# Linear attention and a token-mixing MLP: third products moved, flips and output products on the whole TensorE array, stores held back

## The chip, the cores and the metric

The kernel runs on one core of one Trainium2 chip. A time is the device time of one execution in microseconds; a kernel's time is the median over its runs. A profile is one execution of the program recorded by the hardware profiler. In the profile PE is TensorE's matmul, PEld its weight load, DVE VectorE, ACT ScalarE, POOL GpSimd and SP SyncE, which here only issues DMAs.

## The reference

Two layers follow each other. The first is a causal linear attention with a decay per head, over 4 batches, 8 heads, 768 positions and 64 channels, in blocks of 64:

```
intra = (q k^T * lam^(i-j) for i >= j) v
inter = (q * lam^(i+1)) kv_state
out   = intra + inter
kv_state = lam^64 * kv_state + (k * lam^(63-j))^T v
```

The second takes the result as x [4, 768, 512] (the heads side by side) and mixes tokens:

```
wq = x w_q ; wk = x w_k                      # [4, 768, 64]
mixed = (wq wk^T / 8) x                      # over the 768 positions
out = relu(mixed) w_out                      # [4, 768, 512], float32
```

All inputs and the output are float32.

## The kernel before

The work is tiled into 16 **pairs** n = 0 to 15: batch b = n // 4 and two heads (kk = n % 4). The kernel works in chunks of 128 positions, six to a pair, with both heads packed on TensorE: head 0 on one half of the array's rows or columns, head 1 on the other. The decay is split into a factor on q and a factor on v, so that a mask of zeros and ones is all that is left of it between a query and a key. One iteration of the loop `for n in range(N)` (line 515) does, for pair n:

- `scores(n)` (L275): k^T q for each chunk, four PSUM tiles `sc`; two row halves of the array (the profile writes 64*128).
- `masks(n, a)` (L295): DVE multiplies two of these tiles by the mask, to `pr` in SBUF.
- `inter(n)` (L301): the product of the running state `gs` and the queries, into `oa` (quarters of the array, 64*64).
- `values(n)` (L318): v times `pr`, added into `oa` (two column halves, 128*64); ACT then copies `oa` to `xT`, x transposed.
- `states(n)` (L248): the running sums of k^T v of a pair (128*64), which DVE brings to SBUF as `gs`.
- `turn(n)` (L208): q and k of a coming pair are transposed on TensorE (128*64). DVE writes `qT`, ACT writes `kT`.
- `flip(n - 1)` (L344): `xT` of the pair before is transposed back, in 12 column halves, to `xp`; DVE (for batch 0 ACT) copies it to `xnat`.

When a batch is through, the token mixing of that batch is spread over the pairs of the next two: `mix_wk` (whole array, 128*128), `mix_wq` and `mix_py` (128*64), the third products `mix_pm` (four of them per batch, index dd), and six output products `mix_po` (index t, 128 positions each). A third product has two shapes: wide, two products on two row halves (64*128), or in quarters, four products on 64*64. Two PSUM tiles `pm` come out of it, and ACT applies the relu to both (`rmT`). An output product is eight matmuls in column halves; ACT copies its tile `po` to `osb`, and SP stores 256 KB.

Which of these stands where is written by hand: for each n the lists `rows` (third products ahead of the scores, wide), `quarters` (third products right behind `inter`), `one` (ahead of or behind the turning) and `two` (after `values` and `states`). `tc.manual_schedule()` keeps each engine's instructions in the order of the program. The order in an iteration is

```
before, n < 8:   rows | scores masks0 [wk] states masks1 flip | one turn | inter quarters | values [states] | two
before, n >= 8:  rows | scores masks0 [wk] masks1 | inter quarters | flip turn | one | values states | two
```

PSUM has six buffers that all tiles but `oa` share (`ps`, L51) and two for `oa` (`psx`). A tile that finds no free buffer waits for the evacuation of an earlier one. `osb` has four buffers (L50). Loads of q, k and v are POOL's (float32 in memory, bf16 in SBUF): iteration n issues those of pair n + 6 in the order q, k, scaling of v of pair n + 4 on POOL, v (L201). SP's queue holds, after the loads at the start, nothing but stores.

Of the kernel before, what the change touches and what calls it, by code (L numbers as in the profile page):

```python
# [27 lines left out]
def kernel(  # L28
# [18 lines left out]
    gsp = ctx.enter_context(tc.tile_pool(name="gsp", bufs=3))  # L47
    xtp = ctx.enter_context(tc.tile_pool(name="xtp", bufs=2))
    hyp = ctx.enter_context(tc.tile_pool(name="hyp", bufs=2))
    outp = ctx.enter_context(tc.tile_pool(name="outp", bufs=4))  # L50
    ps = ctx.enter_context(tc.tile_pool(name="ps", bufs=6, space=bass.MemoryType.PSUM))  # L51
    psx = ctx.enter_context(tc.tile_pool(name="psx", bufs=2, space=bass.MemoryType.PSUM))
    ctx.enter_context(tc.manual_schedule())
# [136 lines left out]
    def scale_v(n, eng):  # L190
        b, kk = pairs[n]
        vn = nat.tile([128, 2, NCH, D], BF16, tag="vn", name="vn")
        eng.tensor_tensor(  # L193
            out=vn,
            in0=staged.pop((n, "v")),
            in1=DvI[:, 2 * kk : 2 * kk + 2, :].unsqueeze(3).to_broadcast([128, 2, NCH, D]),
            op=ALU.mult,
        )
        L[n]["vn"] = vn
# [95 lines left out]
    def masks(n, a):  # L295
        for hl in range(2):
            t = prb.tile([128, 3, CH], BF16, tag="pr", name="pr")
            nc.vector.tensor_tensor(out=t, in0=L[n]["sc"][a, hl], in1=maskc, op=ALU.mult)  # L298
            L[n]["pr"][a, hl] = t
# [41 lines left out]
                nc.scalar.copy(out=to, in_=oa[a])  # L341
        del L[n]

    def flip(n):  # L344
        b, kk = pairs[n]
        xp = pst([128, NCH, CH], BF16, "xp")
        for t in range(NCH):
            for i in range(2):
                o = t * CH + i * 64
                nc.tensor.transpose(  # L350
                    xp[i * 64 : i * 64 + 64, t, :], xT[b][:, kk, o : o + 64], ident
                )
        to = xnat[b][:, :, kk * CH : (kk + 1) * CH]
        if b == 0 or n == N - 1:
            nc.scalar.copy(out=to, in_=xp)
        else:
            nc.vector.tensor_copy(out=to, in_=xp)
# [7 lines left out]
    def mix_wk(b, kts=range(NP)):  # L365
        if 0 in kts:
            M[b] = dict(wk=pst([128, NCH, DHY], F32, "wk"))
        wk = M[b]["wk"]
        for t in range(NCH):
            for kt in kts:  # L370
                nc.tensor.matmul(
                    wk[:, t, :],
                    xT[b][:, kt, t * CH : (t + 1) * CH],
                    wqk[:, 1, kt, :],
                    start=(kt == 0 and (t == 0 or len(kts) == NP)),
                    stop=(kt == NP - 1),
                    skip_group_check=True,
                )
        if NP - 1 in kts:
            wkn = hyp.tile([128, NCH, DHY], BF16, tag="wkn", name="wkn")  # L380
            nc.vector.tensor_copy(out=wkn, in_=wk)
            M[b]["wkn"] = wkn

    def mix_wq(b, kts=range(NP)):
        if 0 in kts:
            M[b]["wq"] = pst([128, HALF], F32, "wq")
        wq = M[b]["wq"]
        for kt in kts:
            for n in range(2):
                nc.tensor.matmul(  # L390
                    wq[n * 64 : n * 64 + 64, :],
                    wqk[:, 0, kt, :],
                    xT[b][:, kt, n * HALF : (n + 1) * HALF],
                    start=(kt == 0),
                    stop=(kt == NP - 1),
                    skip_group_check=True,
                )
        if NP - 1 in kts:
            wqT = hyp.tile([128, HALF], BF16, tag="wqT", name="wqT")
            nc.scalar.copy(  # L400
                out=wqT.rearrange("j (c p r) -> j c r p", c=3, r=2),
                in_=wq.rearrange("j (c r p) -> j c r p", c=3, r=2),
            )
            M[b]["wqT"] = wqT

    def mix_py(b, last=False):
        py = pst([128, 256], F32, "py")
        for t in range(NCH):
            for i in range(2):
                nc.tensor.matmul(  # L410
                    py[i * 64 : i * 64 + 64, :],
                    M[b]["wkn"][:, t, :],
                    xnat[b][:, t, i * 256 : i * 256 + 256],
                    start=(t == 0),
                    stop=(t == NCH - 1),
                    skip_group_check=True,
                )
        Y = hyp.tile([128, 2, 256], BF16, tag="Y", name="Y")
        nc.scalar.copy(out=Y[:, 0, :], in_=py)
        for i in range(2):  # L420
            o = slice(64 - i * 64, 128 - i * 64)
            if last:
                nc.vector.tensor_copy(out=Y[i * 64 : i * 64 + 64, 1, :], in_=py[o, :])
            else:
                nc.scalar.copy(out=Y[i * 64 : i * 64 + 64, 1, :], in_=py[o, :])
        M[b]["Y"] = Y
        M[b]["rmT"] = hyp.tile([128, 4, S], BF16, tag="rmT", name="rmT")

    def mix_pm(b, which, wide=True, engs=None):
# [20 lines left out]
        for i, ((dd, n), pm) in enumerate(zip(which, pms)):  # L450
# [10 lines left out]
            else:  # L461
                nc.scalar.activation(out=to, in_=pm, func=ACT.Relu, scale=1.0 / 8.0)  # L462

    def mix_po(b, t, last=False):
        cols = (256, 256) if last and t == NCH - 1 else (HD,)
        osb = outp.tile([128, HD], F32, tag="osb", name="osb")
        c = 0
        for w in cols:
            po = pst([128, w], F32, "po")
            for kt in range(4):  # L470
                for i in range(2):
                    o = t * CH + i * 64
                    nc.tensor.matmul(  # L473
                        po[i * 64 : i * 64 + 64, :],
                        M[b]["rmT"][:, kt, o : o + 64],
                        wo[:, kt, c : c + w],
                        start=(kt == 0),
                        stop=(kt == 3),
                        skip_group_check=True,
                    )  # L480
            if last and (c or (t % 2 and len(cols) == 1)):
                nc.vector.tensor_copy(out=osb[:, c : c + w], in_=po)  # L482
            else:
                nc.scalar.copy(out=osb[:, c : c + w], in_=po)  # L484
            (nc.scalar if len(cols) == 2 and c == 0 else nc.sync).dma_start(
                out=out[b, t * CH : (t + 1) * CH, c : c + w], in_=osb[:, c : c + w]
            )
            c += w


    warm(WARM2)
# [23 lines left out]
    for n in range(N):  # L515
        b, kk = pairs[n]
        if 8 <= n + 6 < N:
            load_more(n + 6)
        if n + 6 >= N and n + 4 < N:
            scale_v(n + 4, nc.gpsimd)  # L520
        if n == 1:
            load_wqk()
        if n == 3:
            nc.scalar.copy(out=wqk, in_=wqk_f)
        p = b - 1

        def po(b, *ts):
            return [lambda t=t: mix_po(b, t) for t in ts]

        rows, quarters, one, two = {
            4: ([], [], [lambda: mix_wq(0)], [lambda: mix_py(0)]),
            5: ([], [0, 1], [], []),
            6: ([2], [3], [], po(0, 0, 1)),
            7: ([], [], po(0, 2, 3), po(0, 4, 5)),
        }.get(n, ([], [], [], []))
        if b >= 2:
            rows, quarters, one, two = [
                ([], [], [lambda: mix_wq(p)], [lambda: mix_py(p)]),  # L540
                ([], [0], po(p - 1, 3) if b > 2 else [], po(p - 1, 4) if b > 2 else []),
                ([1], [2], po(p - 1, 5) if b > 2 else [], []),
                ([3], [], [], po(p, 0, 1, 2) if b < B - 1 else po(p, 0, 1)),
            ][kk]
        for dd in rows:
            mix_pm(p, dd)
        scores(n)
        masks(n, 0)
        if b >= 1 and kk == 0:
            mix_wk(p)  # L550
        if n < 8:

            states(n)
            masks(n, 1)
            if n >= 1:
                flip(n - 1)
            for f in one:
                f()
            turn(n + 1)
            if n == 0:  # L560
                scale_v(1, nc.vector)
                make_dq(2)
            if n == 1:
                make_dq(3)
        else:
            masks(n, 1)

        inter(n)
        for dd in quarters:
            mix_pm(p, dd, wide=False)  # L570
        if n >= 8:
            flip(n - 1)
            if 8 <= n <= 9:
                turn(n + 1)
            if n != 8 and n + 2 < N:
                turn(n + 2)
            for f in one:
                f()
        if n == N - 1:
            mix_wk(b, (0, 1, 2))  # L580
            mix_wq(b, (0, 1, 2))
        values(n)
        if n >= 7 and n + 1 < N:
            states(n + 1)
        for f in two:
            f()
    bl = B - 1
    mix_po(bl - 1, 2)
# [44 lines left out]
```

## Time and profile before

| what | value |
|---|---|
| median of 5 runs | 105.45 us (104.69 to 105.56) |
| profiled execution: own time, span | 105.45 us, 103.4 us |
| PE, PEld busy | 86.5 us, 60.3 us |
| DVE, ACT, POOL busy | 66.2 us, 63.8 us, 67.5 us |
| granted TensorE clock | 1.0 in all slices |
| scores(0) start, scores(8) start, last matmul starts | 9.1 us, 47.8 us, 99.5 us |

A busy PE means that some matmul was in flight, and a matmul on a half or a quarter of the array runs beside its partner. So what a block of matmuls costs TensorE is read from the start of its first matmul to the start of the next block. The timeline gives these starts; a bracket behind a line tells how long the engine stood before it and what ended that. Blocks are named by the tile that they write: `sc` scores, `oa` inter (64*64) and values (128*64), `xp` flip, `trq` and `trk` turning, `dps` states, `pm` third products, `po` output products.

### The profile page before, as it was taken

Reading aid. Unit: us, or ns where it says so; the run is one execution under the profiler, and the core shown is the slowest. Engines: PE = TensorE matmul, PEld = TensorE weight load, DVE = VectorE, ACT = ScalarE, POOL = GpSimd, SP = SyncE. Lnnn points to the kernel's source line nnn. Section 1 sums busy time; section 2 is a strip of 40 time slices with the busy share of each in tenths; the row PEclk is TensorE's granted clock in tenths of the full one; section 3 lists DMA queues with packets and bytes.
Section 4 is the critical chain, followed back from the end, with each engine's and each line's share of the span. In section 5 each row is a group of like instructions: output and inputs, shape, how many; then the busy total and the mean of one; then the engine's idle time right before and its main releaser. Section 6 shows DMA issues by size and latency. Waiting matters only on the chain. (4 is left out here: it accounts for less than half of the span.)

```text
span 103.4 us, 3945 instructions
## 1 busy us (share of the span) xinstructions
PE 86.5 (84%) x1714; PEld 60.3 (58%) x1714; DVE 66.2 (64%) x165; ACT 63.8 (62%) x126; POOL 67.5 (65%) x69
## 2 busy tenths in 40 slices
PE   4955887959886889999798698999899889999950
PEld 1324576746865565786675576768585565643530
DVE  3247998894847493864959399739857782264330
ACT  4283658946491869482397578653888824876430
POOL 5999999898999699999908999996041000000000
PEclk9999999999999999999999999999999999999999
DMA  0999999999999999999999999999903120733584
GB/s 23 267 173 156 163 171 159 175 166 163 195 176 164 164 153 163 124 245 263 199 218 218 158 164 137 136 157 288 153 10 142 67 101 0 270 139 133 220 312 148
DMA packets 67410, 17.15 MB, mean 166 GB/s; under 512 B 62914, under 2 KB 64450, under 8 KB 67394
## 3 DMA queue, kind: packets, MB, share of 16 engines
q0 software_dynamic: 60400, 9.57, 125.1%
q1 hardware_dynamic: 6850, 7.21, 21.4%
q8 instruction: 13, 0.21, 0.8%
q10 hardware_dynamic: 144, 0.13, 0.4%
q14 instruction: 3, 0.02, 0.1%
HBM read 20.19 MB, written 6.29 MB: 256 GB/s over the span
## 5 line engine op out<-in xcount | busy, mean ns | idle before, releaser
L298 DVE TENSOR_TENSOR pr<-sc,maskc 128x384 bf16<-128x384 f32 x64 | 32.0, 548 | 11.7 <-PE sc L285 11.7
L193 POOL TENSOR_TENSOR vn<-fv,DvI 128x768 bf16<-128x768 bf16 x14 | 20.9, 1494 | 9.2 <-DMA fv<-in_v_dram 8.4
L473 PE MATMUL po<-wo,rmT 128*64 128x512 bf16 (+1 forms) x200 | 23.0, 371 | 0.1
L242 ACT COPY kT<-trk 128x768 bf16<-128x768 bf16 x16 | 12.8, 799 | 13.8 <-PE trk L238 13.5
L484 ACT COPY osb<-po 128x512 f32<-128x512 f32 (+1 forms) x22 | 12.6, 582 | 9.9 <-PE po L473 6.0
L79 POOL DMA_DIRECT2D fv<-in_v_dram x16 | 17.3, 1079 | 0.8 <-POOLq L617 0.8
L79 POOL DMA_DIRECT2D fk<-in_k_dram x15 | 15.6, 1037 | 0.0
L473 PEld LDWEIGHTS <-rmT 128*64 128x64 bf16 x200 | 10.8, 110 | 8.0 <-ACT rmT L462 0.7
L341 ACT CAST xT<-oa 128x384 bf16<-128x384 f32 x31 | 13.5, 495 | 2.5 <-PE oa L329 2.5
L462 ACT ACTIVATE rmT<-pm 128x384 bf16<-128x384 f32 x28 | 12.3, 507 | 1.5 <-PE pm L442 1.5
L285 PE MATMUL sc<-qT,kT 64*128 64x128 bf16 x192 | 9.8, 217 | 3.8 <-ACT rmT L462 1.0
L74 POOL DMA_DIRECT2D fq<-in_q_dram x15 | 12.6, 843 | 0.0
L285 PEld LDWEIGHTS <-kT 64*128 64x128 bf16 x192 | 6.6, 94 | 7.7 <-issue 4.6
L225 DVE TENSOR_TENSOR qT<-trq,dq 128x768 bf16<-128x768 bf16 x16 | 8.8, 548 | 1.7 <-PE trq L219 1.7
L238 PE MATMUL trk<-ident,fk 128*64 128x128 bf16 x180 | 7.8, 220 | 2.3 <-DMA fk<-in_k_dram 2.3
L350 PE MATMUL xp<-ident,xT 128*64 128x128 bf16 x192 | 8.4, 221 | 1.0 <-ACT osb L484 0.6
L329 PE MATMUL oa<-pr,vn 128*64 128x128 bf16 x192 | 8.7, 221 | 0.5 <-DVE pr L298 0.5
L219 PE MATMUL trq<-ident,fq 128*64 128x128 bf16 x192 | 8.5, 220 | 0.7 <-ACT fq L501 0.6
L329 PEld LDWEIGHTS <-vn 128*64 128x64 bf16 x192 | 6.7, 109 | 2.5 <-issue 1.3
L308 PE MATMUL oa<-qT,gs 64*64 64x128 bf16 x160 | 7.8, 222 | 0.2
L265 DVE COPY two<-dps 128x64 f32<-128x64 f32 x16 | 3.5, 221 | 6.6 <-PE dps L255 6.5
L350 PEld LDWEIGHTS <-xT 128*64 128x64 bf16 x192 | 6.3, 110 | 2.3 <-issue 1.7
(59 smaller groups left out, 113.2 us busy)
## 6 DMA issues: line engine op xcount, KB each, us to landing
out_dram<-osb SPq DMA_DIRECT2D x23, 256.0 KB, 2.1
fv<-in_v_dram POOLq DMA_DIRECT2D x16, 192.0 KB, 6.6
fq<-in_q_dram POOLq DMA_DIRECT2D x15, 192.0 KB, 7.1
fk<-in_k_dram POOLq DMA_DIRECT2D x15, 192.0 KB, 7.5
wo<-in_moe_w_out_dram POOLq DMA_DIRECT2D x1, 512.0 KB, 9.1
k<-in_k_dram SPq DMA_DIRECT2D x1, 384.0 KB, 3.7
q<-in_q_dram SPq DMA_DIRECT2D x1, 384.0 KB, 4.8
wqk_f<-in_moe_w_q_dram SPq DMA_DIRECT2D x1, 128.0 KB, 6.7
```

The costliest lines, as they stand in the source:

```text
L74: nc.gpsimd.dma_start(out=t, in_=q_rows(n))
L79: nc.gpsimd.dma_start(out=t, in_=kv_rows(n, dict(k=k, v=v)[nm]))
L193: eng.tensor_tensor(out=vn, in0=staged.pop((n, "v")), in1=DvI[:, 2 * kk : 2 * kk + 2, :].unsqueeze(3).to_broadcast([128, 2, NCH, D]), op=A ...
L242: nc.scalar.copy(out=kT, in_=trk)
L285: nc.tensor.matmul(sc[a, hl][:, cc, :], kT[r, c * CH : (c + 1) * CH], qchunk(n, r, c), start=True, stop=True, skip_group_check=True,)
L298: nc.vector.tensor_tensor(out=t, in0=L[n]["sc"][a, hl], in1=maskc, op=ALU.mult)
L329: nc.tensor.matmul(oa[a][r, cc, :], vn[:, hl, c, :], pr[a, hl][:, cc, :], start=False, stop=(cc == 2), skip_group_check=True,)
L341: nc.scalar.copy(out=to, in_=oa[a])
L350: nc.tensor.transpose(xp[i * 64 : i * 64 + 64, t, :], xT[b][:, kk, o : o + 64], ident)
L462: nc.scalar.activation(out=to, in_=pm, func=ACT.Relu, scale=1.0 / 8.0)
L473: nc.tensor.matmul(po[i * 64 : i * 64 + 64, :], M[b]["rmT"][:, kt, o : o + 64], wo[:, kt, c : c + w], start=(kt == 0), stop=(kt == 3), ski ...
L484: nc.scalar.copy(out=osb[:, c : c + w], in_=po)
```

## The change

Four things are changed.

- Third products: the list `rows` is gone. All stand behind `inter`, in quarters: dd 0 and 1 in the pair kk = 1, dd 2 and 3 in the pair kk = 2 (for batch 0 in pairs 5 and 6).
- Output products: a whole-array form, four matmuls of 128 output rows in place of eight on column halves, everywhere. In the loop they stand ahead of `inter` (list `whole`), and for batch 0 all in pairs 7 and 8 (before: 6 and 7).
- Flips: in the pairs from 8 on they stand right behind the scores, the masks and `mix_wk`, and `flip` makes six transposes on the whole array. The flips called in pairs 1 to 7 keep the column halves (`halves=True`). `flip(N - 1)` at the end is whole too.
- Stores: `mix_po` notes its store in a list, and `store()` issues what is noted. For batch 0 nothing is issued at once. At n = 8 SP issues a small DMA that reads v of pair 14 from its staging tile, and so waits until that load has landed; the stores noted so far follow, and the other two of batch 0 go with the first one of batch 1. `osb` gets 14 buffers.

The order in an iteration becomes

```
after, n < 8:   scores masks0 [wk] whole states masks1 flip [wq] turn | inter quarters | values [states] | cols
after, n >= 8:  scores masks0 [wk] masks1 flip whole | inter quarters | turn [wq] | values states | cols
```

where `cols` holds `mix_py` alone.

```diff
-    outp = ctx.enter_context(tc.tile_pool(name="outp", bufs=4))
+    outp = ctx.enter_context(tc.tile_pool(name="outp", bufs=14))
...
-    def flip(n):
+    def flip(n, halves=False):
         b, kk = pairs[n]
         xp = pst([128, NCH, CH], BF16, "xp")
         for t in range(NCH):
-            for i in range(2):
-                o = t * CH + i * 64
-                nc.tensor.transpose(
-                    xp[i * 64 : i * 64 + 64, t, :], xT[b][:, kk, o : o + 64], ident
-                )
+            w = 64 if halves else CH
+            for i in range(0, CH, w):
+                o = t * CH + i
+                nc.tensor.transpose(xp[i : i + w, t, :], xT[b][:, kk, o : o + w], ident)
...
+    stores = []
+
+    def store():
+        while stores:
+            b, t, c, w, osb = stores.pop(0)
+            (nc.scalar if w < HD and c == 0 else nc.sync).dma_start(
+                out=out[b, t * CH : (t + 1) * CH, c : c + w], in_=osb[:, c : c + w]
+            )
+
     def mix_po(b, t, last=False):
...
             for kt in range(4):
-                for i in range(2):
-                    o = t * CH + i * 64
-                    nc.tensor.matmul(
-                        po[i * 64 : i * 64 + 64, :],
-                        M[b]["rmT"][:, kt, o : o + 64],
-                        wo[:, kt, c : c + w],
-                        start=(kt == 0),
-                        stop=(kt == 3),
-                        skip_group_check=True,
-                    )
+                nc.tensor.matmul(
+                    po,
+                    M[b]["rmT"][:, kt, t * CH : (t + 1) * CH],
+                    wo[:, kt, c : c + w],
+                    start=(kt == 0),
+                    stop=(kt == 3),
+                )
...
-            (nc.scalar if len(cols) == 2 and c == 0 else nc.sync).dma_start(
-                out=out[b, t * CH : (t + 1) * CH, c : c + w], in_=osb[:, c : c + w]
-            )
+            stores.append((b, t, c, w, osb))
             c += w
+        if b > 0:
+            store()
...
+        if n == 8:
+
+            late = consts.tile([1, D], BF16, name="late")
+            nc.sync.dma_start(out=late, in_=staged[n + 6, "v"][0:1, 0, 0, :])
+            store()
...
-        rows, quarters, one, two = {
-            4: ([], [], [lambda: mix_wq(0)], [lambda: mix_py(0)]),
-            5: ([], [0, 1], [], []),
-            6: ([2], [3], [], po(0, 0, 1)),
-            7: ([], [], po(0, 2, 3), po(0, 4, 5)),
-        }.get(n, ([], [], [], []))
-        if b >= 2:
-            rows, quarters, one, two = [
-                ([], [], [lambda: mix_wq(p)], [lambda: mix_py(p)]),
-                ([], [0], po(p - 1, 3) if b > 2 else [], po(p - 1, 4) if b > 2 else []),
-                ([1], [2], po(p - 1, 5) if b > 2 else [], []),
-                ([3], [], [], po(p, 0, 1, 2) if b < B - 1 else po(p, 0, 1)),
+        whole, quarters, cols = {
+            4: ([], [], [lambda: mix_py(0)]),
+            5: ([], [0, 1], []),
+            6: ([], [2, 3], []),
+            7: (po(0, 0, 1, 2, 3), [], []),
+            8: (po(0, 4, 5), [], [lambda: mix_py(p)]),
+        }.get(n, ([], [], []))
+        if n > 8:
+            whole, quarters, cols = [
+                ([], [], [lambda: mix_py(p)]),
+                (po(p - 1, 3) if b > 2 else [], [0, 1], []),
+                (po(p - 1, 4, 5) if b > 2 else [], [2, 3], []),
+                (po(p, 0, 1, 2) if b < B - 1 else po(p, 0, 1), [], []),
             ][kk]
-        for dd in rows:
-            mix_pm(p, dd)
         scores(n)
         masks(n, 0)
+
         if b >= 1 and kk == 0:
             mix_wk(p)
+        if n >= 8:
+            masks(n, 1)
+            flip(n - 1)
+        for f in whole:
+            f()
         if n < 8:
 
             states(n)
             masks(n, 1)
             if n >= 1:
-                flip(n - 1)
-            for f in one:
-                f()
+                flip(n - 1, halves=True)
+            if kk == 0 and b:
+                mix_wq(p)
             turn(n + 1)
...
-        else:
-            masks(n, 1)
 
         inter(n)
         for dd in quarters:
             mix_pm(p, dd, wide=False)
         if n >= 8:
-            flip(n - 1)
             if 8 <= n <= 9:
                 turn(n + 1)
             if n != 8 and n + 2 < N:
                 turn(n + 2)
-            for f in one:
-                f()
+            if kk == 0:
+                mix_wq(p)
...
         values(n)
         if n >= 7 and n + 1 < N:
             states(n + 1)
-        for f in two:
+        for f in cols:
             f()
```

## The prediction

> **What bounds the kernel now.** I read the page first, then the timeline of PE from 34 us on, then that of ACT, DVE and POOL beside each stall.
>
> ```profile
> PE 86.5 (84%) x1714; PEld 60.3 (58%) x1714; DVE 66.2 (64%) x165; ACT 63.8 (62%) x126; POOL 67.5 (65%) x69
> ...
> PE   4955887959886889999798698999899889999950
> ...
> DMA  0999999999999999999999999999903120733584
> ```
>
> No engine is full, PE is nearest, and the DMA engines are full for the first three quarters. So PE's order of work sets the time, with holes in it. An undisturbed stretch of PE's timeline gives the price of the blocks and of a change of array form:
>
> ```profile
> 68.47 0.51 PE L285 MATMUL sc<-qT,kT 64*128 64x128 bf16 x12
> 68.91 0.87 PE L371 MATMUL wk<-wqk,xT 128*128 128x64 bf16 x24
> 69.71 0.47 PE L308 MATMUL oa<-qT,gs 64*64 64x128 bf16 x10
> 70.11 0.53 PE L350 MATMUL xp<-ident,xT 128*64 128x128 bf16 x12
> 70.47 0.50 PE L219 MATMUL trq<-ident,fq 128*64 128x128 bf16 x12
> ```
>
> From start to start: scores 0.44, wk 0.80, inter 0.40, a flip 0.36. Within `sc` a pair of matmuls follows the last after 0.053, so six pairs are 0.32, and 0.12 is the change of form behind them. The 24 wk start 0.0295 apart, 0.71, which leaves 0.09; inter costs 0.30 where a 64*64 block follows (53.72 to 54.02) and 0.40 here. A change of form is 0.10.
>
> The holes, from pair 6 to 15:
>
> ```profile
> 50.13 0.53 PE L350 MATMUL xp<-ident,xT 128*64 128x128 bf16 x12 [0.62 <-ACT osb L484]
> ...
> 57.40 0.53 PE L238 MATMUL trk<-ident,fk 128*64 128x128 bf16 x12 [0.73 <-DMA fk<-in_k_dram]
> ...
> 59.57 0.34 PE L285 MATMUL sc<-qT,kT 64*128 64x128 bf16 x5 [0.29 <-DVE gs L267]
> ...
> 74.52 0.35 PE L442 MATMUL pm<-wqT,Y 64*64 64x384 bf16 x3 [0.32 <-ACT Y L425]
> ...
> 83.13 0.32 PE L285 MATMUL sc<-qT,kT 64*128 64x128 bf16 x5 [0.80 <-ACT rmT L462]
> ```
>
> Most are scores that stop halfway. Six PSUM buffers go round, the row-shaped third product ahead of the scores takes two, and the last scores need a buffer that ACT or DVE still empties.
>
> **The change part by part.** I add the starts of the blocks up pair by pair, before and after. The loop from the third product at 35.51 to the end of the output products of pair 15 (two of the three from 85.71, so 87.42) takes 51.9 us; 44.6 of it are blocks at their undisturbed price, 7.3 are waits.
>
> *Third products.* A row one costs 0.17 (62.36 to 62.53), one in quarters 0.16 (inter with it 79.30 to 79.86, 0.56, less 0.40). PE gains nothing by the shape. The scores behind rows took 0.98, 0.95, 0.95, 0.87 and 1.44 in pairs 6, 10, 11, 14, 15 against 0.44, and the flip of pair 6 waited 0.46 for `rmT`: 3.5 us of the 7.3 go. The third products of pairs 9 and 13 stand 0.6 and 0.7 waiting for `Y`; a flip (and in 13 an output product) now covers most of that. With the smaller holes of pairs 10 and 11 these are 1.7 us. With 0.7 and 1.4 further down that is the 7.3.
>
> What is late next: two third products in one pair take four buffers at once. In pairs 9 and 10 the second to fourth wait for masks, and `trk` for the evacuation of the flip. DVE does four masks in 1.95 us from 0.38 behind the scores, and `xnat` after them (53.66 to 56.07 behind scores at 53.28), so `trk` can't start before 2.8 us into the pair; by its blocks PE is there after 1.9 (0.44, flip 0.43, inter 0.40, 0.32, `trq` 0.33). That is 0.9 twice. In pair 13 the output product behind the flip takes the buffer that the copies to `Y` free, 1.3 us in (73.13 to 74.46) where PE is there after 0.9: 0.4, so 2.2 us. Pair 6 gets what pair 5 has now, 1.30 for inter and two third products (33.75 to 35.05) against 0.72, and DVE's chain of masks, states, masks, flip, `qT` behind it: 0.9.
>
> *Flips and output products.* The column halves already stream in pairs: 24 of L473 start 0.213 a pair apart (65.78 to 68.47 for three products, 0.853 each without the change of form). Four whole matmuls of 512 columns can't be under 4 x 0.213; the nearest row above is two whole 512-column warm-up matmuls, 0.226 apart at 6.5 us. So an output product is 0.853 to 0.904, and I take 0.853, by the row with the same operands; the other end is +1.2 us over 24. A whole flip is between 6 x 0.053 and 6 x 0.059 (twice a wk), 0.32 to 0.35 against 0.33 to 0.36: nothing. LDWEIGHTS of 128 columns hides under 0.0295, as wk shows.
>
> The order scores, whole, inter, halves has a form more than scores, inter, halves. Pairs 8 and 12 have wk there anyway; pairs 7, 9, 10, 11, 13, 14, 15 pay 0.10 each, +0.7. The price of a flip is 0.03 less in each of pairs 8 to 15, so the work grows by 0.4. At the end, po, flip, wq, wk, po, py, po, pm, po, pm, po changes form nine times, not six: +0.3 on the path.
>
> The trace shows 0.10 for a change. [...]
>
> [...]
>
> Moved ahead of `inter`, the flip needs the last `xT` 0.5 us after the scores start. ACT does four `rmT` (0.87 per two), `kT` (0.80) and `xT` (0.87) in line in pairs 9, 10, 13 and 14; counted from where their products end, `xT` of 13 and 14 is ready 1.5 us into the next pair, so 0.6 to 0.7 is waited in pairs 14 and 15, 0.1 in 11, and wk waits 0.3 in 12: 1.5 us. In pair 7 four output products stand ahead of `states`; DVE then has states, two masks, flip and `qT` (0.62 + 0.94 + 0.47 + 0.47) in line when scores(8) is due: 0.4. Output products behind the values covered that before.
>
> *Stores.* SP waits at n = 8 for v of pair 14, with all stores of batches 0 and 1 that follow queued behind, nothing else. ACT no longer waits for an `osb` buffer:
>
> ```profile
> 49.49 0.59 ACT L484 COPY osb<-po 128x512 f32<-128x512 f32 x1 [1.82 <-DMA out_dram<-osb]
> ...
> 54.54 1.47 POOL L193 TENSOR_TENSOR vn<-fv,DvI 128x768 bf16<-128x768 bf16 x1 [2.69 <-DMA fv<-in_v_dram]
> ```
>
> The first hole goes (0.7). By the trace's landings the loads come 1.1 to 1.25 us apart until 43.7, and the next six, beside six stores, take 6.4 us more than at that rate. With the stores gone k of pair 11 lands by some 52, not 57.4, and POOL's 2.69 go; the turning of pair 9 saves 1.4. From there POOL's own 4.33 us a pair (57.03 to 61.37) sets the loads.
>
> Held stores come back: v of pair 14, issued 2.7 sooner, lands by 67, and nine stores meet q, k, v of pair 15. Alternating one to one (six loads beside six stores, as above), k lands near 71.6; `turn(15)` wants it near 74 in my sum. Hidden by 2 us; v is wanted 5 us later. The small DMA costs a slot on SP alone.
>
> **Sum.** Waits from 7.3 to 5.0 (0.9 pair 6, 0.4 pair 7, 2.2 buffers, 1.5 `xT`), work +0.4, end +0.3: -1.6 on the profiled run's own 105.45 (span 103.4 and 2.05 around it), which is also the median: **103.9**.
>
> **The rivals.** *The waits mostly hide.* The whole forms ahead of `inter` give DVE and ACT 0.4 to 2.6 us a pair, and the buffer that a tile gets may be an older one than I assumed. If half of the 5.0 goes, 101.4; if all, 98.9, the floor of the sum. Against it: DVE's masks and flip are in line in every pair.
>
> *The flip becomes the wait.* Each of the eight flips in pairs 8 to 15 stands for ACT's `xT`, as the flip at 50.13 stands now for ACT: 1.08 from inter to it against 0.40, 0.68 more. Eight times that is 5.4 against 1.5 for `xT` in my sum, so 107.8. It is slower than before by over 0.5% from a mean of 0.45 a flip. For it: ACT's line of rmT, kT, xT; against it: pairs 8, 9 and 12 have no third product ahead of it.
>
> *The stores come back as the wait.* Three stores per load and not one would put k of pair 15 at 75.8, 1.8 late: 105.7, no change. For it: three stores at 67.5 to 69.2 delayed four loads by 3.0 us; against it: the six at 41.6 to 50.1 shared evenly.
>
> **How the numbers follow.** My case 0.60, hidden waits 0.15, the flip 0.15, the stores 0.10. Half a per cent, 0.53 us, is about what a measurement of this kernel can tell from no change. My own case spans 102.8 (output waits in 9, 10, 13 halved) to 105.1 (whole products at 0.226), a tenth of it within 0.5%; the slow flip in part as well. Faster 0.70, same 0.14, slower 0.16. The range takes the half of the hidden waits at the low end, and the upper end stops short of the full flip: 101.3 to 106.1.
>
> **What would show it.** Scores 0.44 in every pair from 6 on (third products right); a flip in pairs 8 to 15 of 0.32 to 0.35 behind a gap of 0.10; whole output products 0.213 a matmul; `xp` idle for ACT `xT` in pairs 11, 14 and 15, `trk` for DVE `xnat` in 9 and 10; no POOL hole near 52; scores(9) near 52.9, scores(12) near 66.7, the end of pair 15 near 85.5. The forecast is wrong if the flips wait over 0.5 each, if whole products are slower than 0.226, or if `trk` of pair 15 stands for its load.

## The result, and the profile after

The changed kernel takes 106.73 us, the median of 43 runs (105.81 to 109.1); the kernel before took 105.67 over 80 runs beside it. The ratio is 1.0115, with a 95% interval of 1.0096 to 1.0134: slower. (Ratios here and below leave disturbed executions out, so they need not be the quotient of the medians.) The forecast was 103.9, faster. The profiled execution of after took 106.46 us with a span of 104.5.

The page of after, the rows that answer to those shown of before:

```profile
PE 90.4 (86%) x1570; PEld 59.2 (57%) x1570; DVE 65.8 (63%) x165; ACT 63.6 (61%) x126; POOL 67.6 (65%) x69
...
PE   4986998967976989999999888999897989999960
...
DMA  0999999999999999999999999999930405132584
```

PE has 144 instructions less and is busy 3.9 us longer, in part because PE counts as busy while a matmul is in flight and the next one waits (below, a flip of 0.51 is busy 0.72). The slices say little. The starts of the scores say where the time is:

| pair | 6 | 7 | 8 | 9 | 10 | 11 | 12 | 13 | 14 | 15 | sum |
|---|---|---|---|---|---|---|---|---|---|---|---|
| before | 5.65 | 6.47 | 5.48 | 5.61 | 3.64 | 5.93 | 4.67 | 5.29 | 3.52 | 5.48 | 51.7 |
| after | 4.49 | 7.08 | 6.40 | 4.37 | 4.42 | 5.83 | 4.98 | 4.45 | 5.14 | 5.67 | 52.8 |
| my sum for after (not on record in this split) | 3.83 | 7.0 | 6.4 | 4.5 | 3.95 | 5.3 | 4.95 | 4.25 | 4.65 | 5.05 | 49.9 |

(From scores to scores in us; pair 15 to the end of its last block, output products before, values after. Of the last row the prediction itself gives the starts of scores(9) and scores(12) and the end, 52.9, 66.7 and 85.5; the split between them was worked out from its terms afterwards.) Before and after can't be compared pair by pair, since third and output products have moved. From the start of scores(8) to the last flip it is 40.50 before and 42.13 after, and in that stretch after has two output products more (1.72): what the removed holes gave is used up by new waits and by the changes of form. Before scores(8) after wins 0.55 with 1.72 of work left over, so 1.2 is lost there.

The holes of the kernel before are gone. Its waits of PE from 35 to 88 us, the three longest, were

```profile
PE sc L285 <- ACT rmT L462: 1.0, 2, 0.8
PE trk L238 <- DMA fk<-in_k_dram: 0.7, 1, 0.7
PE xp L350 <- ACT osb L484: 0.6, 1, 0.6
```

and those of after, from 35 to 90 us, are

```profile
PE xp L351 <- ACT xT L341: 2.1, 5, 0.8
PE pm L441 <- ACT kT L242: 0.5, 2, 0.2
PE pm L441 <- ACT rmT L461: 0.4, 1, 0.4
PE po L479 <- ACT Y L424: 0.4, 1, 0.4
```

One line took the place of three: the flip waits for ACT's `xT`. The 2.1 are the idle time only, and one of the five is a flip that was not moved, in pair 6 (0.29). From start to start the waits for `xT` in the pairs from 8 on cost 3.8 us. PE's timeline of after gives it, pair 9 first, where nothing waits:

```profile
53.64 0.51 PE L285 MATMUL sc<-qT,kT 64*128 64x128 bf16 x12
54.08 0.51 PE L351 MATMUL xp<-ident,xT 128*128 128x128 bf16 x6
54.52 0.47 PE L308 MATMUL oa<-qT,gs 64*64 64x128 bf16 x10
...
58.02 0.51 PE L285 MATMUL sc<-qT,kT 64*128 64x128 bf16 x12
58.89 0.72 PE L351 MATMUL xp<-ident,xT 128*128 128x128 bf16 x6 [0.37 <-ACT xT L341]
59.55 0.35 PE L308 MATMUL oa<-qT,gs 64*64 64x128 bf16 x6
...
63.24 0.73 PE L351 MATMUL xp<-ident,xT 128*128 128x128 bf16 x6 [0.30 <-ACT xT L341]
...
77.70 0.57 PE L285 MATMUL sc<-qT,kT 64*128 64x128 bf16 x12
79.03 0.72 PE L351 MATMUL xp<-ident,xT 128*128 128x128 bf16 x6 [0.76 <-ACT xT L341]
79.59 1.89 PE L479 MATMUL po<-wo,rmT 128*128 128x512 bf16 x8
...
84.15 0.73 PE L351 MATMUL xp<-ident,xT 128*128 128x128 bf16 x6 [0.43 <-ACT xT L341]
```

In pair 10 the flip starts 0.87 behind the scores and the next block 0.66 behind the flip, where those of pair 9 take 0.44 and 0.44: 0.65 lost, 0.2 of it inside the flip, whose second half waits for the second half of `xT`. The same reckoning gives 0.60 in pair 11, 0.30 for `mix_wk` of pair 12 (it reads `xT` too), 1.11 in pair 14 and 1.10 in pair 15, where the scores stop 0.3 for a buffer too, inside the time for which `xT` is late anyway. The sum is 3.8, of which the moved flips have 3.46.

Why `xT` is late is in ACT's timeline of after around scores(10), at 58.02, and scores(14), at 77.70:

```profile
55.42 1.64 ACT L461 ACTIVATE rmT<-pm 128x384 bf16<-128x384 f32 x4 [0.45 <-PE pm L441]
56.92 1.53 ACT L242 COPY kT<-trk 128x768 bf16<-128x768 bf16 x2
58.30 0.92 ACT L341 CAST xT<-oa 128x384 bf16<-128x384 f32 x2
...
76.26 1.64 ACT L461 ACTIVATE rmT<-pm 128x384 bf16<-128x384 f32 x4
77.76 0.83 ACT L242 COPY kT<-trk 128x768 bf16<-128x768 bf16 x1
78.44 0.92 ACT L341 CAST xT<-oa 128x384 bf16<-128x384 f32 x2
```

From the first `rmT` on ACT works without a gap. Two third products hand it four `rmT` at once; `kT` and `xT` stand behind them, and the last `xT` is there 1.2 us into pair 10 and 1.66 into pair 14. The flip, 0.44 behind the scores, is the first to need it.

### The profile page after: what moved, and what is told of

Its sections match the earlier page's. It is cut to its first block, busy times and chain, and to the rows that moved or that the text cites. A ratio compares the mean times of both kernels' runs of the same rounds, so it can differ in the third digit from the quotient of the medians.

```text
span 104.5 us, 3653 instructions
## 1 busy us (share of the span) xinstructions
PE 90.4 (86%) x1570; PEld 59.2 (57%) x1570; DVE 65.8 (63%) x165; ACT 63.6 (61%) x126; POOL 67.6 (65%) x69
## 4 chain that ended last, share of the span: by engine, by line
PE 42%; ACT 18%; DMA 17%; POOL 14%; DVE 3%; issue 2%; POOLq 0%; ACTq 0%
PE po L479 20%; DMA fk<-in_k_dram 9%; DMA fv<-in_v_dram 7%; ACT rmT L461 7%; ACT kT L242 6%; PE xp L351 5%; POOL fv L79 4%; POOL fq L74 3%; ACT xT L341 3%; POOL fk L79 3%; PE oa L308 3%; PE wk L370 2%; PE trk L238 2%; PE pm L441 2%; PE trq L219 2%
## 5 line engine op out<-in xcount | busy, mean ns | idle before, releaser
L479 PE MATMUL po<-wo,rmT 128*128 128x512 bf16 (+1 forms) x100 | 22.7, 371 | 0.5 <-ACT Y L424 0.4
L479 PEld LDWEIGHTS <-rmT 128*128 128x128 bf16 x100 | 9.1, 98 | 10.5 <-issue 1.3
L461 ACT ACTIVATE rmT<-pm 128x384 bf16<-128x384 f32 x28 | 11.7, 498 | 1.5 <-PE pm L441 1.5
L285 PE MATMUL sc<-qT,kT 64*128 64x128 bf16 x192 | 9.2, 224 | 3.0 <-issue 1.4
L351 PE MATMUL xp<-ident,xT 128*64 128x128 bf16 (+1 forms) x138 | 9.4, 222 | 2.4 <-ACT xT L341 2.1
L329 PE MATMUL oa<-pr,vn 128*64 128x128 bf16 x192 | 9.2, 227 | 0.2 <-DVE pr L298 0.2
L219 PE MATMUL trq<-ident,fq 128*64 128x128 bf16 x192 | 9.2, 232 | 0.1
L351 PEld LDWEIGHTS <-xT 128*64 128x64 bf16 (+1 forms) x138 | 5.8, 105 | 4.8 <-ACT xT L341 4.2
L219 PEld LDWEIGHTS <-fq 128*64 128x64 bf16 x192 | 6.9, 117 | 2.2 <-DVE fq L505 0.8
```

The lines of the kernel that those rows point to most:

```text
L219: nc.tensor.transpose(trq[hl * 64 : hl * 64 + 64, a, r, :], fq[:, hl, a, r * D : (r + 1) * D], ident,)
L285: nc.tensor.matmul(sc[a, hl][:, cc, :], kT[r, c * CH : (c + 1) * CH], qchunk(n, r, c), start=True, stop=True, skip_group_check=True,)
L329: nc.tensor.matmul(oa[a][r, cc, :], vn[:, hl, c, :], pr[a, hl][:, cc, :], start=False, stop=(cc == 2), skip_group_check=True,)
L351: nc.tensor.transpose(xp[i : i + w, t, :], xT[b][:, kk, o : o + w], ident)
L479: nc.tensor.matmul(po, M[b]["rmT"][:, kt, t * CH : (t + 1) * CH], wo[:, kt, c : c + w], start=(kt == 0), stop=(kt == 3),)
```

## The experiments

The theory after the result, A in the expectations: putting the flip ahead of `inter` makes it wait for `xT`, and this alone is the loss; the rest of the change gains. The rivals, B to D in the expectations: the whole-array forms cost what is lost; holding the stores does nothing or harms; whatever block stands there would wait, for PSUM buffers.

**Flips back behind the quarters.** After, with the flips of pairs 8 to 15 in column halves again, where they stood before:

```diff
-            flip(n - 1)
         for f in whole:
...
         for dd in quarters:
             mix_pm(p, dd, wide=False)
         if n >= 8:
+            flip(n - 1, halves=True)
```

> The changed kernel with one thing undone: from pair 8 on the flip stands behind the third products again, in column halves, ahead of the turning. Theory A (the flip, moved to right behind the scores, waits for ACT's xT: 0.65, 0.6, 0.3, 1.1 and 1.1 us in pairs 10, 11, 12, 14 and 15 of the changed kernel's profile, 3.8 in all): these waits go, perhaps 1 us of new ones comes at the third products, which lose the flip's cover; 2 to 3.5 us under the changed kernel, so 1 to 2% faster than before. Rival B (the whole-array form and its added changes of form are what costs): two pairs lose a change of form, 0.2 us, and the kernel stays 0.8 to 1.2% slower than before.

Measured: 103.66 us, 0.970 of before (0.9653 to 0.9747); a second measurement, further down, gave 103.89 and 0.9792. Scores(8) to the last flip is 38.89, 3.2 us shorter than after: 2.8 of it in pairs 10, 11, 14 and 15, and 0.5 in pair 13, where the flip of after did not wait for `xT`, but the output product behind it waited for a PSUM buffer (the row of `Y` above). PE's timeline of this kernel in pair 14:

```profile
75.72 0.51 PE L285 MATMUL sc<-qT,kT 64*128 64x128 bf16 x12
76.27 1.89 PE L479 MATMUL po<-wo,rmT 128*128 128x512 bf16 x8
78.09 0.36 PE L308 MATMUL oa<-qT,gs 64*64 64x128 bf16 x6
...
78.81 0.53 PE L351 MATMUL xp<-ident,xT 128*64 128x128 bf16 x12
79.17 0.50 PE L329 MATMUL oa<-pr,vn 128*64 128x128 bf16 x12
```

The output products stand 0.55 behind the scores and the flip does not wait. So it is not that any block in this place waits, and theory A holds for most of the loss; pair 13's 0.5 belongs to the rival of the buffers. The edit also takes the whole-array form from the flips, which the next run separates.

**Flip and output products swapped.** After, with the whole flip kept ahead of `inter`, but behind the output products:

```diff
         if n >= 8:
             masks(n, 1)
-            flip(n - 1)
         for f in whole:
             f()
+        if n >= 8:
+            flip(n - 1)
```

> The changed kernel with one pair of calls swapped: in the pairs from 8 on the output products stand ahead of the flip, both still on the whole array and ahead of inter. No change of form is added or taken. Theory A (the flip comes before ACT has written xT): in pairs 11, 13, 14 and 15 an output product or more, 0.86 us each, covers what the flip waits for, and the waits of the changed kernel there (0.6, 0.5, 1.1, 1.1 us) go; pair 10 has no output product and keeps its 0.65. 2 to 3 us under the changed kernel, 1 to 1.7% faster than before. Rival D (a flip anywhere ahead of inter costs, since its buffer waits for DVE behind the four masks): the flip's buffer is still taken ahead of the masks' end, so within 0.7 us of the changed kernel, 0.5 to 1.2% slower than before.

Measured: 104.59, 0.9875 (0.9817 to 0.9934). Only the pairs with output products can change, 8, 11, 13, 14 and 15. Pair 8, whose flip did not wait, stays at 6.40; pair 11 falls from 5.83 to 5.25, pair 13 from 4.45 to 3.90, pair 14 from 5.14 to 4.54, pair 15 from 5.67 to 5.07, 2.3 us in all. (The profiled execution took 105.65, 1.1 over the median; what it lost lies ahead of scores(8).) Pair 14:

```profile
78.10 0.59 PE L285 MATMUL sc<-qT,kT 64*128 64x128 bf16 x12
79.06 1.89 PE L479 MATMUL po<-wo,rmT 128*128 128x512 bf16 x7 [0.37 <-ACT kT L242]
80.78 0.50 PE L351 MATMUL xp<-ident,xT 128*128 128x128 bf16 x6
81.21 0.35 PE L308 MATMUL oa<-qT,gs 64*64 64x128 bf16 x6
```

The same flip, in the same form, 0.43 long: its place was the cost, not its form. The rival of the buffers has a grain of truth: the 0.55 of pair 13 is not a wait for `xT`, and here the output product of pair 14 stands 0.37 for a PSUM buffer that ACT's `kT` empties. Pair 10, which has no output product, keeps its wait.

**`xT` made by DVE.** If ACT's line is the cause, taking `xT` out of it should give back most. After, with both copies to `xT` of pairs 9, 10, 13 and 14 on DVE:

```diff
-            if n == N - 1 and a == 0:
+            if n in (9, 10, 13, 14) or (n == N - 1 and a == 0):
```

> The changed kernel, flips in their new place, with both copies to xT of pairs 9, 10, 13 and 14 made by DVE in place of ACT. Theory A (the flip of the next pair waits for ACT, which has four relu copies and kT ahead of xT): the waits of pairs 10, 11, 14 and 15, 3.4 us in the changed kernel's profile, shrink to well under 1 us, DVE's line grows by 1.1 us in these pairs, where it idles 1 to 2 us; 2 to 3 us under the changed kernel, 0.5 to 1.5% faster than before. Rival D (the place itself costs, through PSUM buffers or through DVE's evacuation of the flip in line with the masks): within 0.5% of the changed kernel, 0.7 to 1.7% slower than before.

Measured: 105.85, 1.0042 of before (0.9992 to 1.0092), 0.7% under after: far less than expected. Pairs 14 and 15 fall by 0.45 and 0.5, pairs 10 and 11 stay. The waits changed owner, as PE's timeline of this kernel shows:

```profile
60.12 1.55 PE L441 MATMUL pm<-wqT,Y 64*64 64x384 bf16 x8
...
64.35 0.39 PE L479 MATMUL po<-wo,rmT 128*128 128x512 bf16 x1 [0.25 <-DVE gs L267]
...
79.19 0.50 PE L351 MATMUL xp<-ident,xT 128*128 128x128 bf16 x6 [0.37 <-DVE two L265]
```

In pair 14 the flip now waits for a buffer that DVE's `two` frees late, as DVE has made `xT` first; in pair 11 the output product waits for DVE's `gs`; and the third products of pair 10 are strung out over 1.55 us. I read the wait as one for the whole evacuation behind PE, ACT and DVE together. Here moving a copy between them moved the wait; moving the consumer away, as in the two runs before, removed most of it.

**The forms alone.** Before, with output products and the flips from pair 8 on in whole form at their old places:

```diff
-                for i in range(2):
-                    o = t * CH + i * 64
-                    nc.tensor.matmul(
-                        po[i * 64 : i * 64 + 64, :],
+                nc.tensor.matmul(
+                    po,
...
-                flip(n - 1)
+                flip(n - 1, halves=True)
```

(The second place is the call in the pairs below 8; `flip` is that of after.)

> The kernel before with the whole-array form of output products and of the flips from pair 8 on, each at its old place. There are some 22 more changes of form than before. If each costs the 0.10 us that I read off the trace of before, and a whole output product 4 x 0.216: +2.5 us, 2 to 2.5% slower than before. If changes of form cost nothing on the path: +0.3 us, within 0.5%. If they cost 0.2: +4.5 us, 4% slower. By theory A, which blames the place and not the form, this run says nothing of the flip's wait: no xp idles for xT here.

Measured: 105.82, 0.9991 (0.9952 to 1.0031): no change, where 2 to 2.5% were expected. The price is in the blocks, as PE's timeline of this kernel shows:

```profile
74.39 0.51 PE L351 MATMUL xp<-ident,xT 128*128 128x128 bf16 x6
74.83 0.53 PE L219 MATMUL trq<-ident,fq 128*64 128x128 bf16 x12
75.19 0.50 PE L238 MATMUL trk<-ident,fk 128*64 128x128 bf16 x12
75.62 1.04 PE L470 MATMUL po<-wo,rmT 128*128 128x512 bf16 x4
76.59 0.53 PE L329 MATMUL oa<-pr,vn 128*64 128x128 bf16 x12
```

A flip takes 0.44 and not 0.36, an output product 0.97 and not 0.87, and the turning ahead of it 0.43 and not 0.33: 0.10 for each change. But this kernel lost the two holes of before, for `osb` (0.7) and for k of pair 11 (0.7): its pair 8 began 1.1 us later, after a standstill of 0.73 at 38.9 of the kind told in the last section, and the loads were there. Against the next kernel, which has no such holes either, its scores(8) to the last flip is 39.36 against 38.42: the forms cost 0.9 us, and a hole hid it. (That rests on one profile of each.) The forms are not the loss of after, but they are no gain either.

**The stores.** Before, with 14 buffers and the held stores:

```diff
-    outp = ctx.enter_context(tc.tile_pool(name="outp", bufs=4))
+    outp = ctx.enter_context(tc.tile_pool(name="outp", bufs=14))
...
+            stores.append((b, t, c, w, osb))
             c += w
+        if b > 0:
+            store()
...
+        if n == 8:
+            late = consts.tile([1, D], BF16, name="late")
+            nc.sync.dma_start(out=late, in_=staged[n + 6, "v"][0:1, 0, 0, :])
+            store()
```

> The kernel before with the stores' part alone: 14 osb buffers, stores of batch 0 held until v of pair 14 has landed. By the prediction's step the hole of 0.7 us in pair 8 and the 1.4 us at the turning of pair 9 go and nothing else changes: 103.4 to 104, 1.5 to 2% faster than before. Rival C (what is gained is taken back by the next wait, since the third products of pairs 10 and 11 wait for ACT and DVE anyway, or by the stores beside pair 15's loads): under 0.5% either way.

Measured: 103.03, 0.9758 (0.9678 to 0.9839). Both holes are gone in PE's timeline of this kernel: pair 8 has 4.67 for 5.48, pair 9 4.23 for 5.61.

```profile
48.94 0.47 PE L308 MATMUL oa<-qT,gs 64*64 64x128 bf16 x10
49.33 0.53 PE L350 MATMUL xp<-ident,xT 128*64 128x128 bf16 x12
...
55.06 0.50 PE L219 MATMUL trq<-ident,fq 128*64 128x128 bf16 x12
55.39 0.50 PE L238 MATMUL trk<-ident,fk 128*64 128x128 bf16 x12
```

These are the flip and the turning that stood 0.62 and 0.73 before. So holding is no harm: this part alone is worth 2.4%. Before with the 14 buffers alone (the first two lines of the diff):

> The kernel before with 14 osb buffers and nothing else. The wait of ACT for an osb buffer goes, and with it the 0.7 us hole of pair 8: 0.5 to 0.8% faster than before. By the step that gave the rest to the loads, k of pair 11 lands as late as before and the turning of pair 9 still waits 1.4 us and more. If the buffers alone bring the 2.4% of the run of the stores' part, holding the stores does nothing.

Measured: 105.29, 0.9994 (0.9951 to 1.0037). Pair 8 gets its 0.8 back, and the time does not change; it is the holding that gains. (Where the 0.8 goes can't be read: the profiled execution took 107.32, 2 us over the median, with two of the standstills told in the last section.) After, with the stores issued at once:

```diff
-        if b > 0:
-            store()
+        store()
...
-        if n == 8:
-            late = consts.tile([1, D], BF16, name="late")
-            nc.sync.dma_start(out=late, in_=staged[n + 6, "v"][0:1, 0, 0, :])
-            store()
```

> The changed kernel with the stores not held: each is issued as soon as its osb is there, with 14 buffers. If holding is worth its 1.4 us in this order too, k of pair 11 lands near 57 and the turning of pair 9 waits again: 0.5 to 1.5 us over the changed kernel, 1.7 to 2.5% slower than before. By rival C nothing changes: 1 to 1.3% slower than before.

Measured: 107.73, 1.0162 (1.0114 to 1.0209), 0.5% over after, with intervals that overlap. k of pair 11 lands at 54.9 instead of 51.5, still ahead of its turning: in the order of after the load is no wait. The same edit on the kernel with the flips back, twice:

> The kernel with the flips put back (3% faster than before) and stores issued at once, 14 buffers. If holding the stores is what makes it fast, as the run of the stores' part alone suggests: 1.5 to 2.4 us slower than with holding, 0.7 to 1.5% faster than before. If holding is worth little once the output products of batch 0 stand in pairs 7 and 8 with buffers enough, as the changed kernel without holding suggests (0.5%): 2.3 to 3% faster than before, and the rest of its gain is the order of third and output products.

> The kernel with the flips put back and the stores issued at once, a second time. In the profiles, code fetch stalls left out, it takes the pairs 6 to 15 as fast as with holding (50.0 against 50.3 us). If the profile is right, 2.5 to 3.5% faster than before, as with holding; if holding has a worth of its own that a single profile does not show, 1 to 2%.

Measured: 104.46 with no usable interval, then 104.71, 0.9898 (0.9841 to 0.9956), beside the repeat of the first experiment on the same chip:

> The kernel with the flips put back behind the third products, a second time, to stand beside the next two on one chip: 2.5 to 3.5% faster than before.

Measured: 103.89, 0.9792 (0.9728 to 0.9855). So holding is worth some 1.1% here, though these two intervals overlap a little, and 2.4% in the order of before. Where the 1.1% comes from is open; the last section has what the profiles suggest.

**Output products spread.** The flips back, and the two output products of pair 8 moved to pairs 9 and 10, which have none:

```diff
-            8: (po(0, 4, 5), [], [lambda: mix_py(p)]),
+            8: ([], [], [lambda: mix_py(p)]),
...
-                (po(p - 1, 3) if b > 2 else [], [0, 1], []),
-                (po(p - 1, 4, 5) if b > 2 else [], [2, 3], []),
+                (po(p - 1, 3) if b > 2 else po(0, 4), [0, 1], []),
+                (po(p - 1, 4, 5) if b > 2 else po(0, 5), [2, 3], []),
```

> The kernel with the flips put back, and the last two output products of batch 0 moved from pair 8 to pairs 9 and 10, ahead of inter. There PE waits 1.0 us (for Y, then masks) and 1.1 us (for gs, xT, rmT) in the profile of the kernel with the flips put back. Each product is 0.86 us of work. If it fills these waits: 1 to 1.6 us less, 4 to 4.5% faster than before. If the chain of DVE and ACT behind the scores just moves along with it: within 0.5% of the 3%.

> The kernel with the flips put back and the last two output products of batch 0 in pairs 9 and 10, a second time. Its profile has pairs 8 to 10 in 13.5 us against 14.9, but lost as much to stalls on code ahead of pair 6. If those stalls are chance, 1 us less than with the flips put back alone, 3.5 to 4.5% faster than before; if they belong to where its blocks of code begin, equal to it.

Measured: 102.69, 0.9733 (0.9671 to 0.9795), and 103.03, 0.9754 (0.9709 to 0.98). The output product stands where PE waited for `Y` and the masks. PE's timeline of the second:

```profile
53.38 0.51 PE L285 MATMUL sc<-qT,kT 64*128 64x128 bf16 x12
53.82 1.04 PE L479 MATMUL po<-wo,rmT 128*128 128x512 bf16 x3
54.79 0.35 PE L308 MATMUL oa<-qT,gs 64*64 64x128 bf16 x6
```

Scores(8) to the last flip is 37.55 in the profile of the first and 38.19 in that of the second (which has one of the standstills of the last section in it), 1.3 and 0.7 less than with the flips back alone, with the same work; the total does not tell the two apart. This version, the flips back without it, and the held stores alone in the order of before all beat both kernels, by 2 to 3% of before, and their intervals overlap.

## Why the prediction was wrong, by its steps

Its mechanisms were there, and its sum failed in one term, the waits for `xT`. The end of pair 15 was put at 85.55 and came at 88.51, 3.0 us late; the end and the time around the span came out 0.4 shorter than I had them. By the table, pairs 7, 8, 9 and 12 came out within 0.13 us; 2.1 of the 3.0 are pairs 10, 11, 14 and 15, 0.7 is pair 6, 0.2 pair 13. Pair 6's part is a wait for `xT` too.

- **The waits for `xT` (the failed step).** I put 1.5 us on them; 3.8 were measured from pair 8 on. Part of that is arithmetic. In pairs 14 and 15 the step had the line of ACT right and its length nearly (the last `xT` 1.5 us into pair 14; measured 1.66), but an `xT` that is needed at 0.5 and ready at 1.5 costs 1.0, not the 0.6 to 0.7 that I wrote; 1.11 and 1.10 were measured. And the four terms as written add up to 1.6 to 1.8, not 1.5. With 1.0 twice the step would have been 2.4 and the forecast 104.8. The rest is a wait that I did not see: for pair 10 I had none and for pair 11 0.1; they were 0.65 and 0.60. There the line was miscounted: pair 9 turns two pairs, so ACT has two `kT` in it, 1.53 us and not 0.80, and the late third products (ACT idle 0.45 ahead of `rmT`) push the whole line on. I had priced the buffers of pairs 9 and 10 as a delay of `trk`, and did not carry that delay through ACT to the next flip.
- **The rival that came true in kind** is the flip as the wait. Its point of decision, 0.45 a flip, is 3.6 us over eight; 3.8 were measured with `mix_wk`'s 0.30, 3.46 or 0.43 a flip without. Its own price, 0.68 for all eight, was too much: what I held against it, that some pairs have no third products ahead, is right for pairs 8 and 9, whose flips do not wait. The swap of flip and output products shows that the place decides. None of the three signs by which the forecast was to be called wrong came: the mean stayed under 0.5 a flip, though two flips waited 1.1.
- **Pair 6**: 0.9 predicted, 1.6 measured. The third products cost what I had taken (1.30 from inter to the values); the excess is the flip of pair 5, which lost 0.64 waiting for `xT`, behind four `rmT` on ACT. I had counted DVE's chain alone. It is the same omission.
- **The row-shaped third products**: right. The twelve scores of each pair from 6 to 14 start without a stop; the stops of up to 0.8 are gone, but for 0.3 in pair 15.
- **The buffers**: 2.2 us, in size right: some 0.8 in pair 9 (4.37 for 4.5) and 0.8 in pair 10, and 0.6 in pair 13, where the output product waits for `Y` and I had 0.4. They appear at `pm`, not at `trk`. In pair 10 the wait for `xT` comes on top.
- **The forms**: 0.10 a change, right in the loop (with the forms alone the turning ahead of an output product took 0.43 for 0.33, the product 0.97 for 0.87); the 0.3 that I added at the end did not show (from the end of pair 15 to the end of the span 16.0 both before and after). Of the matmuls I misread the row: 0.213 is from the second half of a pair to the first of the next, and the pairs start 0.216 apart (39.505 to 41.016 in seven steps). A whole output product runs at 0.2158 a matmul, so the two forms cost the same, as I had taken it. The twelve weight loads of the flip of before at 70.11 start two by two, 0.003 apart, and the pairs 0.056 apart, the last 0.25 behind the first in a flip of 0.36.
- **Stores and loads**: right in each part. k of pair 11 landed at 51.5, the 2.69 us hole of POOL is gone, the stores went out from 66.9 and the turning of pair 15 at 76.3 waited for nothing. The rival of the stores fell. But little of the 2.1 us that I gave to it shows in the order of after, 0.5% by the run with the stores issued at once. SP's own queue shows the hold, 50.9 us of waiting for v:

```profile
SPq L529 <- DMA fv<-in_v_dram: 50.9, 1, 50.9
```

- **What would have been right**: with the flips where they were, and all else as changed, 103.66 and 103.89 were measured. That my total of 103.9 agrees with theirs is chance: it has 1.5 us in it for the moved flips, which these kernels don't have.

## What to carry to other kernels

When a block is moved forward, ask for each input not whether it is computed by then but when the engine that evacuates it gets to it: write that engine's whole line out, every instruction that the pair puts into it, and carry each delay into the next pair. Here a block whose inputs had long been ready, an output product, did better behind the scores, and the block with the freshest input behind it (pair 14 in 4.54 us and not 5.14). A change of several parts can hide a gain of 2.4% (the held stores) behind a loss of 3 to 4% (the order), so try the parts alone; and a price that one kernel hides in a hole, as the forms' price seems to have been, can fall due when the hole is closed.

## What the hardware showed that was not expected

**TensorE stands still at fixed places of its program.** In every profile PE stands still, without any semaphore, at some of the same places in its program, 256 instructions or a multiple of it apart, give or take one (weight loads and matmuls counted): numbers 705, 962, 1218, then 1728, 1984, 2241 and 2497. The profile calls it "issue" (once it names DVE, see below). The DMA queue named "instruction" has 12 or 13 transfers of some 16 KB in each execution; around these places one starts when PE has some 30 to 130 instructions left up to the place, mostly 50 to 80, takes 0.9 to 1.1 us beside the loads, and PE goes on 1.3 to 1.8 us after its end. In before, such a transfer ran from 28.87 to 29.76, and PE stood 0.81 until 31.36. PE's timeline of the repeat with the flips back:

```profile
25.88 0.32 PE L285 MATMUL sc<-qT,kT 64*128 64x128 bf16 x5 [1.16 <-issue]
...
32.15 0.23 PE L285 MATMUL sc<-qT,kT 64*128 64x128 bf16 x1 [1.16 <-issue]
...
38.90 0.41 PE L238 MATMUL trk<-ident,fk 128*64 128x128 bf16 x7 [1.03 <-issue]
```

That PE waits there for its own code, as two of the expectations have it, is read from this coincidence of places and transfers; no run tested it. What a standstill costs, only the runs show: 0.2 to 1.3 us each, 0.8 to 4.5 us in a profile, and differently from one execution to the next: the two profiles with flips back and stores at once have 1.5 and 4.5. In three profiles the granted clock then fell to 0.5 for 3.4 us: in the first of the spread output products from 26.3, where 1.34 at instruction 705 ended, in the swap from 26.7, with the buffers alone from 65.1 (mean clock 0.983, 0.984 and 0.984). In the first of these `mix_wk` took 1.40 to the next block, in after 0.81. Standstills of 1.16, as above, were not always followed by it, and no run shows that they bring it about. So a single profile can be some us longer than another for this alone.

The stretch from scores(8) to the last flip is free of them in every kernel for which it is given above, with one exception, the second run of the spread output products. There the profile names DVE's `gs`, which `mix_py` does not read; the place is instruction 1729, and the same block ran through in the first run:

```profile
52.61 0.84 PE L409 MATMUL py<-xnat,wkn 128*64 128x256 bf16 x11 [0.35 <-DVE gs L266]
```

**Stores beside loads may add to the standstills.** The kernel with the flips back and stores at once has two such places more, in the stretch where its stores run:

```profile
53.92 0.39 PE L255 MATMUL dps<-vn,fk 128*64 128x64 bf16 x7 [0.22 <-issue]
...
60.39 0.27 PE L255 MATMUL dps<-vn,fk 128*64 128x128 bf16 x3 [1.16 <-issue]
```

With the stores held, the same blocks of the program run through (the states at 58.52, the scores at 58.90). The other profile of it shows one at 58.06, after with stores at once at 59.32, before with 14 buffers alone at 57.71 and 64.46; of the eight profiles with held stores one has one between 45 and 66 us, the 52.61 above. But the kernel before and the one with the forms alone, which store at once too, have none there either. And the profile shown here is of an execution of 105.49, 0.8 over its median. It could account for the 1.1% that holding is worth where no load is waited for; it rests on single profiles, and no run changed the code's place or size alone, so it is argued, not shown.
